# An attention and MLP kernel on one core: planner thresholds set for each half group of score blocks, and a new order of instructions

## The chip, the core and the metric

The kernel runs on one core of one Trainium2 chip. Its engines work side by side, each on its own list of instructions: TensorE (PE in the profile; its weight loads are PEld), VectorE (DVE), ScalarE (ACT), GpSimd (POOL) and SyncE (SP), which starts transfers. The metric is the time in device microseconds of one launch; 746.28 us is the median of three runs before the change.

## What is computed

The reference mixes an attention block A and an MLP block B of the same input `x` (1 x 2048 x 640, bf16) by a gate:

```python
def _A_ref(x, wqkv, wo):
    B, S, D = x.shape
    H = 32; Dh = D // H
    qkv = (lambda x, *d: x.transpose(*d))((x @ wqkv).reshape(B, S, 3, H, Dh), 2, 0, 3, 1, 4)
    q, k, v = qkv[0], qkv[1], qkv[2]
    scale = Dh ** -0.5
    scores = jnp.einsum("bhqd,bhkd->bhqk", q, k) * scale
    p = _softmax(scores, axis=-1)
    o = jnp.einsum("bhqk,bhkd->bhqd", p, v)
    return (lambda x, *d: x.transpose(*d))(o, 0, 2, 1, 3).reshape(B, S, D) @ wo

def _B_ref(x, w1, b1, w2):
    h = jnp.einsum("bsd,df->bsf", x, w1) + b1
    sp = jnp.log1p(jnp.exp(-jnp.abs(h))) + jnp.where(h > 0, h, jnp.zeros_like(h))
    act = h * jnp.tanh(sp)
    return jnp.einsum("bsf,fd->bsd", act, w2)

x = A_x
g = _sigmoid((x * gate_w).sum(-1, keepdims=True))
return g * _A_ref(x, A_wqkv, A_wo) + (1 - g) * _B_ref(x, B_w1, B_b1, B_w2)
```

The 32 heads have 20 dimensions each; the MLP is 640 to 1536 to 640 with the Mish function.

## The kernel before

**Tiles.** Four heads form a quad, and 512 queries a column block. A group (`GROUPS`, L52) is one quad with one column block: 8 x 4 = 32 groups, the first 24 quad by quad, the last 8 (quads 6 and 7) column block by column block. A group has 64 score blocks: 16 stretches of 128 keys for each of four heads, each block 128 keys by 512 queries, so 2,048 blocks in all. A half group is 32 blocks.

**One block.** TensorE computes its scores with one matmul on 32 of the array's rows (a head's 20 dimensions, padded), into one of seven PSUM banks (`emit_score`, through `mm`, L506, whose call stands at L507 in the profile). One to four blocks, one for each row tile, go out side by side as a score group. The exponential is then taken in one of two ways:

- ScalarE takes one, two or three neighbouring banks in one instruction and writes bf16 into one, two or three of the 34 slots of `E` (L1312).
- VectorE takes one bank and writes, as 16-bit integers, a straight line that reads as a power of two in bf16 (`psum_chord`, L1345). Two more terms with other offsets are then derived from it (`line`, L1363), two blocks at a time: by GpSimd (`poll_gp`, L1512), or by VectorE where GpSimd has much to do (`run_x`, L1367). The sum of the three terms stands for the exponential. Such a block therefore occupies three slots of `E`, and its product with V takes three matmuls in place of one.

PV matmuls use 32 of the array's columns, one column tile for each of the quad's four heads, and add up in the eighth bank (`emit_pv`, L1000). Up to four go out side by side as a PV group. V has columns of ones, so the same sum gives the softmax denominator. When a group is complete, VectorE copies the bank out (L1406); its denominators go through DRAM and back, and GpSimd multiplies (L1620).

**Other work.** The transposes of `x`, the projections, the MLP and the output projection are cut into pieces (`Misc`) with due times in units of half groups. They run in TensorE's column shape in between, use the same seven banks, and are mostly evacuated by VectorE.

**What sets the order.** `make_plan` (L422) plays the kernel through with a clock of assumed costs. Whenever an engine is free, its poll function chooses what it does next: `poll_pe` (L1156) tries scores, then PV when few slots of `E` are free, then pieces that are due soon, then PV, then other pieces, and in the end `fill` (L1184), four matmuls with zero weights into the bank of sums. `poll_act` (L1225) chooses the banks for ScalarE, `poll_dve` (L1382) the block for VectorE. The choices depend on thresholds in `PAR`: how many blocks a score group must have (`vk`, `idlek`), when it may be smaller (`thr`, `lead`, `hold`), how much GpSimd may have queued when VectorE begins a new pair (`gpmax`), when a derived term goes to VectorE (`xmin`, `xwait`, `xb`), when ScalarE takes three banks (`a3gp`), how long a PV is held after its exponential (`slack`, in `late`, L1200), how many banks pieces may hold (`mb`), and others.

`late_par` (L877) gives a threshold its value: one before block 591 (`ph`), another (`thr_2` and so on) from there on. `elow`, `urgent` and `swait` have one value throughout.

The plan yields 5,440 steps. `ORDER` (L124) is a fixed text, three hexadecimal digits for each step, that says in which order these steps are written out; `unpack` (L262) reads it and the loop at L1773 emits them. Nothing else orders the engines: each runs its own list, and semaphores between them follow from what the steps read and write.

Of the kernel before, what the change touches and what calls it, by code (L numbers as in the profile page):

```python
# [52 lines left out]
for _c in range(NQC):  # L53
    GROUPS += [(6, _c), (7, _c)]
NG = len(GROUPS)
NU = NG * 64
# [39 lines left out]
    "wo": 23.808422394577885,  # L96
    "thr_2": 337.7597040015291,
# [19 lines left out]
for _k in ("thr", "lead", "gpmax", "xmin", "xwait", "vk", "a3gp", "dahead", "age", "ahd", "hold", "idlek", "mb", "dvw", "slack", "mgb", "xb"):  # L117
# [7 lines left out]
    "007000000000000000000000000000000000000000005000000000000000000000000000000000000000000000000000000000000000000000000000001000"  # L125
    "000000000000000000000000000001000000002001000000000000000000000000001000000000000000000000001000000000000001000000000000001000"
# [4 lines left out]
    "00900800a00000000a00b00000000000000000100300000000d00000400100200300500600700800a00e009000002000002001000001000000003004006002"  # L131
    "00500700800000900b00a00c00d00e00800f01001301401601501201701901801101b01c01e01d01f00000600800700900a00b00c00d00e00f010016014013"
    "01201501a00000800a00000500000a00000200000200000000d000001003002000002001000000003001000004003000006001000006002003005007001000"
    "00500000200500b00000200000200400000600500700200900a00800d00c00b01000e01301101601201501701800f01901b01a01d01c01e01f020021023024"
    "02202502702802a02902c02f02e02b03003703503403303103a03603803903b02d03c03d04003f041042032044053000033032031000022023025027024029"
    "02802a02b02c02e02f03003103203303403803700002101d02302202402502602702802d02a03003102c00002402d02a03002e029031026039033032034035"
    "03600002e02f03403503203703603803903300002a02d02c03002e02f02103303103503a03403203c00002002102200000e01001400000100600500800400b"
    "00700c00300e00a00901001200d00f01501101300000300400500600800700900b00a00c00d00e01201001100001401101201301501901601b00000a01200b"
    "01301100f00000700800000600800900b00a00700d00c00e01001100f01201500000300400000500000400500900e00301000000500600800000000200000c"
    "00300600500b00e00a00900800700f01c01101001201301401601701501901801b01d01f01a01e00001401301a01901801501b016017000000000000000000"  # L140
    "00000100300700500800000a00c00800900b00400000d00b00c00f00500000400800000300000400300e00800900600a00700b01600d01000f011000000001"
    "00000000300200700600900000800900000a00500300600000700000300600100a00200800400f000005002007009000008000000000000001000000000000"
    "00500200000000100000100200000000100000200100000000100000100000100000100000000600100800400000900100a00500800c00300701001300b000"
    "00100000000000000200300900600a00b00c00d00e00101001101301401500000301300101501601b01701400e00401801901a01201c000012013000000001"
    "00300600800000c00800500200a00b00701001100d00e01401500f01301601701801a01201c01d01902702001b02202402301f02502802601e02a02102c02d"
    "02e03002f03202903403503703303803603a03b03c03102b03e03f03904104004404604504704804a04c04e04204d03d04f04905105204b043054053057056"
    "05005905505800005905805a05c05705d06305f06005b06205e06506106406706806a06606906d06c06f06e07007207107507707607307807d07a07c07f079"
    "08208106b08008408508308708807b08a08908b08608e09008d09209409308c08f07409609500009609109409209307809509c09809909a09d0970a309b000"
    "01701300000600500c00000f00700900a00601100801600d01201300c01701801000101f01501b01a01401c02401e02000001400000800a00c00d00e00f000"
    "00c000000000000000001008000000000005003002001006000003002006001004000003004000000000000000000000001000006009001005008002004007"  # L150
    "00d00c00b00e01100a01201301401900f00001300000700800000600700500800900b00a00d00e00c000001000002000003002004006009005019007000002"
    "00400600500300800900700d00a00e00f01401200000100800a00b00c00f00501000e00d00000300800200100500700600d00900f00a01000c00000700e00a"
    "00d01000f012011013000003000000000002001000000001000000000001000000000000000000001000000000000000000000000000000000000000002001"
    "00000100000000000100300400600000300600000000100400200300000000300100200400600a00800c00900500b00d00000b00700800d00a000003005007"
    "006000000002001000000000000000000000001002005003004000001000001000002001003000004000005002004006007000007000002001000000001000"
    "00000000000100200300500400a00900800700d00c00e00600f01101201001601401501701801a01e01b01301c01d02002301f02201902100001901c01a01e"
    "01d02001f02300000600701400900a00c00d00f00e01000b01600000200800100400000400300500100600900700a008000000002006003001005007008009"
    "00a00e00b00c00d01000f01101701201301601901801a01b00001b01a00000800900c00f01100e00d010000012011015016014013017018000000000000000"
    "00100200500400300600700d00c00b01100e00801000f01201301401601501b01702001a01801c01f01d01e02101902302400902502202602802702902c02b"
    "02d02e03002f03103302a00002a02b02e02d03003203303102c00000c00e00f00d01101001301400000e01301100000700b00c00a00501000400d000000001"  # L160
    "00000000000100300500000200600800700500900b00a00c00e00f01000d01201101501401601800001501601700000900000800700a00900600c00b00d010"
    "00f00e01100000000200000000200100300000100000200b00000200300500400700600800e00d00b00c00f00901101201501301401601701901801b01a01d"
    "01c02102001e01f02302502202602400001801701901c01b01e01d02200000500600700902c00a00d00c01400000400600500300800700a00b00c01300e00d"
    "01001401201101500000700000000000100000100300200f00500700001d00500600701000900002300602500002200d00400500e01002d00000100000601b"
    "00200901c00b00100001200700a00001e00700900601602d00b02302401801701902601b02502803402902a02b00c00a01d02c03a01203002e01f02f03c022"
    "02000002900702b01f00000001b00001701501801d01601c01a01e01f02102302202002402602802502700001801902001a01c01d01e01f021022023025024"
    "00000f00c00d00e01001101601201301401501701b01c01901a01802501d01f02302002202602401e02802102702902a02f02b03402e03102c02d030032036"
    "03803503304003c03a03904403b03d03e00003403b03703803a03c04103d02c04204000000e00800d01201301101601700901501400f010000000005001004"
    "00200300800600000300000200300000200100600000200500600000000400900000200000000c00001201400600000701400800000000d001009000014000"
    "00800400600b00700d00f01401501001701600000100a00000d00000300100000100200300000000800f001002011000001014003000003005016004006000"  # L170
    "00600000200000000500c00700d00300100600001701901800000200500100000000200400500100300700600800d00c000005000009000001009000004002"
    "00000600000000700a00000f000001000000000013004005003001006007000003004002000001000007000000000000000000005002003000000000001002"
    "000002000006007000001000010001000001000000000004002001003000000001000003001000000000001002000000000000000001000000002000000000"
    "00000000000100000000500000100200300000000000000200500100300700400000000000000000000000000000300100900c00e005006010008002015019"
    "00b00d00700f00000600d00e00000100800300a00400f00000200400c00600700b00d01100e00000700800b00a00c00f00e00d011013010015012000013017"
    "01501601e01802201901b01c01a00000200300a00400700c01000d00b00f01100600e01701200801301401601801c01901a00001401201601701801d01901a"
    "02101c00001200f01401801601701e01a01301f01901d01b000013017000000000001002000000001000000000001002005004003006000000000000002001"
    "00000000000000000000000000100000200100000400100200300500000000100200000200100000100800300600400900700500b00e00f00d00c010011012"
# [243 lines left out]
def make_plan(K, par):  # L422

    pl = Clock()
# [375 lines left out]
    for c in range(NQC):  # L800
        for f in range(FT):
            k = c * FT + f
# [74 lines left out]
    def late_par(k):  # L877
        return par[k + "_2"] if nxt[0] >= par["ph"] else par[k]
# [277 lines left out]
    def poll_pe():  # L1156
# [649 lines left out]
```

## Time and profile before

| | |
|---|---|
| median of three runs | 746.28 us (745.99 to 746.67) |
| the profiled execution | 747.05 us |
| its span, first to last instruction | 745.1 us |
| score blocks whose exponential ScalarE takes | 1,464 |
| score blocks on VectorE | 584 |
| derived terms (two blocks each) on GpSimd, on VectorE | 431, 153 |
| PV matmuls | 3,216 |

How to read the rows that follow in the prediction. A row of a group names its line, engine, operation, the tiles written and read, their shapes and the count; after the bar stands the time in which at least one of them ran and the mean of one in ns; after the second bar the idle time of the engine just before them, and what ended it. Matmuls that run side by side on different row or column tiles overlap, so a mean of 383 ns is the length of one and not the distance to the next. That distance is read from the rows in order of time, whose first two columns are the start and the length in us; neighbouring matmuls of one form are merged in one row with their count. `E,VA` are PV matmuls, `qT,kT` scores, `xT,zero` fill. A row by stretches gives, after the stretch and its length, the busy us and number of instructions of each engine.

### The profile page before, as it was taken

The page shows a single profiled execution, that of the slowest core. Times are in us where ns is not written, and L with a number is a line of the kernel's source. Part 1 is how long each engine was busy: PE and PEld are TensorE (multiplying, and loading weights), DVE is VectorE, ACT ScalarE, POOL GpSimd, SP SyncE. Part 2 cuts the span into 40 slices and gives each one's busy share as a digit, 9 for nine tenths or more (in the row PEclk, how much of TensorE's full clock was granted, in tenths as well). Part 3 has the DMA queues.
Part 4 walks back from the last instruction along what each step waited for, and adds up shares of the span by engine and source line. Part 5 has one row for each costly group of instructions (what it writes and reads, how often), then busy time and mean ns, then how long its engine had stood idle before and what let it go on. Part 6 is the DMA issues. An engine that isn't in the chain of part 4 may idle for free.

```text
span 745.1 us, 24873 instructions
## 1 busy us (share of the span) xinstructions
PE 729.6 (98%) x10332; PEld 255.2 (34%) x10332; DVE 607.1 (81%) x1047; ACT 713.2 (96%) x750; POOL 521.9 (70%) x501
## 2 busy tenths in 40 slices
PE   8999999999999999999999999999999999999997
PEld 4433343333235333333332222223433333333333
DVE  4688888888979797988788878887878788797876
ACT  6899989999999999999999999999999999999995
POOL 9466735565578557667676587687986788797884
PEclk9999999999999999999999999999999999999999
DMA  9611120011011000112102211130111111211202
GB/s 284 199 48 54 50 82 17 20 52 39 17 29 60 16 29 26 50 44 74 39 28 59 54 43 50 39 101 21 43 52 39 39 38 39 71 60 60 72 21 86
DMA packets 45720, 41.82 MB, mean 56 GB/s; under 512 B 20120, under 2 KB 39240, under 8 KB 45608
## 3 DMA queue, kind: packets, MB, share of 16 engines
q1 hardware_dynamic: 42984, 39.94, 17.8%
q8 instruction: 80, 1.31, 0.7%
q10 hardware_dynamic: 2624, 0.31, 0.3%
q14 instruction: 32, 0.26, 0.1%
HBM read 27.59 MB, written 12.38 MB: 54 GB/s over the span
## 4 chain that ended last, share of the span: by engine, by line
PE 80%; ACT 10%; DVE 7%; issue 2%; POOL 0%; DVEq 0%; ACTq 0%; POOLq 0%
PE ps L507 80%; ACT E L1312 9%; DVE E L1347 4%; DVE E L1365 2%; DVE accs L1406 0%; POOL E L1365 0%; ACT act L1236 0%; PE ps L1753 0%; PE ps L520 0%; ACT xT L528 0%; ACT L1236 0%; DVE bst L656 0%; DVEq L1801 0%; DVE qT L544 0%; DVE ost L689 0%
## 5 line engine op out<-in xcount | busy, mean ns | idle before, releaser
L1312 ACT ACTIVATE E<-ps 128x1024 bf16<-128x1024 f32 (+2 forms) x723 | 680.0, 1070 | 19.3 <-PE ps L507 16.4
L1365 POOL TENSOR_SCALAR E<-E 128x1024 uint16<-128x1024 uint16 x431 | 457.8, 1063 | 209.7 <-DVE E L1347 155.0
L1347 DVE TENSOR_SCALAR E<-ps 128x512 uint16<-128x512 f32 x584 | 388.8, 684 | 94.1 <-PE ps L507 85.6
L507 PE MATMUL ps<-E,VA 128*32 128x512 bf16 x3216 | 299.4, 383 | 1.7 <-DVE E L1347 0.6
L507 PE MATMUL ps<-qT,kT 32*128 32x512 bf16 x2048 | 284.0, 384 | 5.3 <-ACT E L1312 2.6
L507 PEld LDWEIGHTS <-kT 32*128 32x128 bf16 x2048 | 75.3, 91 | 261.3 <-issue 257.2
L507 PEld LDWEIGHTS <-VA 128*32 128x32 bf16 x3216 | 78.9, 95 | 97.5 <-issue 78.2
L1365 DVE TENSOR_SCALAR E<-E 128x1024 uint16<-128x1024 uint16 x153 | 97.9, 643 | 2.0
L507 PE MATMUL ps<-R,act 128*32 128x320 bf16 x1536 | 87.1, 302 | 0.4 <-ACT act L1236 0.4
L507 PE MATMUL ps<-xT,R 128*32 128x512 bf16 x960 | 82.4, 383 | 0.0
L507 PEld LDWEIGHTS <-R 128*32 128x32 bf16 (+1 forms) x1728 | 40.8, 95 | 44.7 <-issue 34.0
L507 PEld LDWEIGHTS <-act 128*32 128x32 bf16 x1536 | 36.4, 95 | 32.1 <-issue 22.2
L637 DVE TENSOR_SCALAR act<-ps,b1f 128x512 bf16<-128x512 f32 x48 | 35.7, 744 | 7.4 <-PE ps L507 6.6
L507 PE MATMUL ps<-wv,xT 128*32 128x241 bf16 (+2 forms) x720 | 37.6, 276 | 0.5 <-DVE E L1347 0.3
L507 PE MATMUL ps<-wk,R 128*32 128x320 bf16 (+1 forms) x640 | 37.5, 303 | 0.2
L507 PE MATMUL ps<-xT,wq 128*32 128x512 bf16 x400 | 34.8, 383 | 0.1
L507 PE MATMUL ps<-xT,wk 128*32 128x512 bf16 (+1 forms) x360 | 34.7, 384 | 0.0
L1620 POOL TENSOR_TENSOR ons<-accs,rb 128x512 bf16<-128x512 f32 x24 | 31.5, 1310 | 1.8 <-DVE E L1347 0.7
L567 DVE CAST stg<-ps 128x512 bf16<-128x512 f32 (+1 forms) x40 | 27.3, 683 | 5.1 <-PE ps L507 4.9
L507 PEld LDWEIGHTS <-xT 128*32 128x32 bf16 (+1 forms) x720 | 19.6, 96 | 13.0 <-issue 9.4
L1406 DVE COPY accs<-ps 128x512 f32<-128x512 f32 x31 | 21.2, 684 | 1.3 <-PE ps L507 1.0
L1236 ACT ACTIVATE act<-act 128x3072 bf16<-128x3072 bf16 x8 | 21.5, 2752 | 0.0
(72 smaller groups left out, 190.3 us busy)
## 6 DMA issues: line engine op xcount, KB each, us to landing
rb<-rd_d SPq DMA_DIRECT2D x124, 64.0 KB
qd<-stg SPq DMA_DIRECT2D x20, 128.0 KB
b_d<-bst SPq DMA_DIRECT2D x16, 160.0 KB
out_dram<-ost SPq DMA_DIRECT2D x16, 160.0 KB
kT<-kd SPq DMA_DIRECT2D x28, 80.0 KB
qT<-qd SPq DMA_DIRECT2D x28, 80.0 KB
stg<-b_d SPq DMA_DIRECT2D x13, 160.0 KB
kd<-stg SPq DMA_DIRECT2D x16, 128.0 KB
```

The costliest lines, as they stand in the source:

```text
L507: K.nc.tensor.matmul(o, lhsT=l, rhs=r, start=first, stop=last, tile_position=pos, skip_group_check=True)
L567: K.nc.vector.tensor_copy(out=K.stg[0:w, s, :], in_=bank(b)[0:w, :])
L637: K.nc.vector.tensor_scalar(out=K.act[:, f, (c % 2) * QC : (c % 2 + 1) * QC], in0=bank(b), scalar1=K.b1f[:, f : f + 1], scalar2=None, op0= ...
L1236: K.nc.scalar.activation(a, a, ACT.Mish)
L1312: lambda: K.nc.scalar.activation(K.E[:, e : e + w, :], K.ps[:, b0 : b0 + w, :], ACT.Exp, scale=SCALE)
L1347: lambda: K.nc.vector.tensor_scalar(out=K.E[:, e + h, :].bitcast(U16), in0=K.ps[:, b, :], scalar1=CH_MUL, scalar2=CH_OFF + CH_ADD[0], op0= ...
L1365: eng.tensor_scalar(out=o, in0=i, scalar1=float(CH_ADD[k]), scalar2=1.0, op0=ALU.add, op1=ALU.mult)
L1406: emit(lambda: K.nc.vector.tensor_copy(out=K.accs[:, g % 2, :], in_=K.ps[:, ACCB, :]))
L1620: gp_q.append((1350.0, lambda: K.nc.gpsimd.tensor_tensor(out=dst(), in0=K.accs[:, b, :], in1=K.rb[:, b, :], op=ALU.mult), lambda: pl.give( ...
```

## The change

`PAR` gets a table `win` with one entry for each half group from 0 to 62, each with 19 thresholds. `late_par` looks up the half group that the next score block belongs to (`nxt[0] // 32`), goes back to an earlier one if there is none, and uses the values of before only where the table has none (`mgb` alone). `elow`, `urgent` and `swait` are now read through `late_par` too. `ORDER` is replaced; the plan has 5,519 steps. All functions that write instructions are as they were.

```diff
@@ PAR @@
+    "win": {
+        0: {"thr": 311.433, "lead": 183.566, "gpmax": 3438.02, "xmin": 2062.55, "xwait": 144.133, "vk": 3, "a3gp": 1688.88, "dahead": 387.745, "age": 6.22086, "ahd": 8.57763, "hold": 5, "idlek": 7, "mb": 9, "dvw": 69.8524, "slack": 141.973, "xb": 3, "elow": 20.6823, "urgent": 22.6857, "swait": 211.87},
...
+        30: {"thr": 125.838, "lead": 56.4012, "gpmax": 6719.54, "xmin": 2767.26, "xwait": 124.546, "vk": 3, "a3gp": 5844.89, "dahead": 236.954, "age": 7.03157, "ahd": 3.79319, "hold": 0, "idlek": 5, "mb": 7, "dvw": 158.838, "slack": 44.9159, "xb": 0, "elow": 48.3964, "urgent": 12.8156, "swait": 91.9349},
...
+        62: {"thr": 103.466, "lead": 46.6119, "gpmax": 6719.54, "xmin": 2590.39, "xwait": 132.388, "vk": 3, "a3gp": 10617.2, "dahead": 223.929, "age": 9.63641, "ahd": 4.29725, "hold": 3, "idlek": 4, "mb": 9, "dvw": 283.517, "slack": 73.7542, "xb": 0, "elow": 60.7258, "urgent": 27.9078, "swait": 75.8091},
+    },
@@ late_par @@
-        return par[k + "_2"] if nxt[0] >= par["ph"] else par[k]
+        w = nxt[0] // 32
+        while w >= 0:
+            if k in par["win"].get(w, ()):
+                return par["win"][w][k]
+            w -= 1
+        return par[k + "_2"] if k + "_2" in par and nxt[0] >= par["ph"] else par[k]
@@ poll_pe @@
-        if len(efree) <= par["elow"] and try_pv():
+        if len(efree) <= late_par("elow") and try_pv():
...
-        if try_misc(par["urgent"]):
+        if try_misc(late_par("urgent")):
@@ poll_act @@
-                if len(at) + len(fl) > 1 and nxt[0] < NU and pl.t < idle_since[0] + par["swait"]:
+                if len(at) + len(fl) > 1 and nxt[0] < NU and pl.t < idle_since[0] + late_par("swait"):
@@ ORDER @@
...
```

More of the change, by code (lines that the diff above doesn't have):

```diff
@@ L124 @@
 ORDER = (
[L125 to L126 removed]
+    "007000000000000000000000000000000000000000000004000000000000000000000000000000000000000000000000000000000000000000000000001000"
+    "000000000000000000000000000001000000002001000000000000000000000002000000000000000000000000001000000000000001000000000000001000"
     "000000000000000000000000000000000001000000000000000000000000000001000000000000000000000000000000000000000000000000000000000000"
@@ L134 @@
[L134 to L137, printed above, removed]
@@ new lines @@
+    "00300600500000500300400700800900600a00d000001004006005007000005000003005004000000000003006000001004000003000001002005004007006"
+    "00000500600800700c00000400000000000000100000100000300500000700000200400700500c00a00f00000300600d00000d00000400500600700300a011"
+    "000000000000005001002000002003000006001000001000001000000002001000000001000000000000000002003000000000000000001009002000009007"
+    "00000300000000200500000000000000200000400200300600c00000000000100200000000100000000000000a002000002003004006007005000000000001"
@@ new lines @@
+    "00200300000000000000400200600300b00c00500800700900a00d00e00101101000f01a01300000200500600400300700900a00b00c00d01000e00f011012"
+    "01300000100200400500000000000000000400000100400601400200000000200000000000100200000100000600000200600900400700800b00a00c00f000"
+    "00f00c00d01001101201301401501601701901c01a01b000008005006007000000002001005004008000003004000001003002004005000002001004003005"
+    "000000000000000000001002000000001000000000000001003000004002000000000000001002003004000007001003005000008006004000005008000002"
@@ new lines @@
+    "006004005000000000000001000000001002000000002003000003000001003002000000000001000000005001002003006000000003000007000000000000"
+    "00100400000500700400f00800900a00b01300c01400e01000000f01400001501601201700000c01501901101601700701801a01c01b01d01e01f020022023"
+    "02502602700000800900a00000900800a00000700900a00800c00b00d00f00e010011013012015016014017018000001002000001003000002003004005000"
+    "00100200300400000200100400500300600700900a00800b00c01100e00000200500300700800900a00000000200500000300200600700a00900b00500f008"
@@ new lines @@
+    "01000d01201501101801601301900000b01000801201400e01100f01301701602201a01901c01d01801e01b02002102402301f02602900002302a025028000"
+    "01601301801e01901f01c01b01d01a02002202302802600000800b00300900a01000c00e00d00f01101300001001101d012014000011015014013017018020"
+    "01601e01c01901d01a01f02102202402600001701b01c01d01e01f021020022019023000001000001003002006005004007008009000002001013003004000"
+    "00201100100400c00000000300200500100000400b00600700000700c00a00800d00e00000a00500600800900701900b00e01200000c00b000001000000000"
@@ new lines @@
+    "00100000100200900500600b00800400700a00d00c00000100200900000300100200000000000000400300200100000200100000c000000001004003005006"
+    "002000000000000000002001003006005007009000004006009008000003007005006008000000000000003000000002000000002000003002004000000001"
+    "000002000000000000000000000000000000001000001000003001006002004005000000000000000000000001000001000001000004001003000005003004"
+    "00600800700900a00b00c00d00f00e000000001005004002003006007000000002000000001000006000001000000000000001000000001002000000000000"
@@ new lines @@
+    "000001002000000000000000000000000000000000000000000000000000000000000000001002000003001002000000000000002001000000000000000000"
+    "00000000000000000100000000500100000100200600400500800700a00900b00c00e00000200000000100000100900200500400600700a00800c00000800a"
+    "00c00000000000000200000500200300400000200300b00100400000500000300100200600000000100300000000000100400500300600900800700a000009"
+    "000002001000000000001004002000002005004006003007008009000001002004000000000000002003005004000005000002003006001004000002003004"
@@ L255 @@
+    "00000000000300200400600501900801a00700900a00d00c00b00f00e00001501101600f01b01a00000700000c00000100000500900800a00d00100e00f011"
+    "00601300000400000e00000500a000000002003000000000000"
 )
```

280 lines of the change are left out of this document (160 added, 120 removed).

## The prediction

> **What bounds the kernel now.** I read the page first (busy shares, slices, chain), then the busy time by stretches, the matmul order in time, the waits, and the groups of instructions. The page:
>
> ```profile
> span 745.1 us, 24873 instructions
> PE 729.6 (98%) x10332; PEld 255.2 (34%) x10332; DVE 607.1 (81%) x1047; ACT 713.2 (96%) x750; POOL 521.9 (70%) x501
> PEclk9999999999999999999999999999999999999999
> PE 80%; ACT 10%; DVE 7%; issue 2%; POOL 0%; DVEq 0%; ACTq 0%; POOLq 0%
> ```
>
> TensorE is busy for 98% of the span and carries 80% of the chain that ended last; ScalarE is close behind. The stretches, cut where the 1st, 129th, 1,665th and last of the 2,048 score blocks start (columns: length, then busy us of each engine with its instruction count, granted clock, DMA share, GB/s):
>
> ```profile
> 0.00:10.40 10.40, 7.83 (x94) 4.36 (x95) 3.10 (x9) 3.86 (x6) 9.73 (x22) 1.00 0.87 284
> 10.40:60.10 49.70, 48.91 (x666) 20.11 (x665) 35.66 (x77) 46.54 (x51) 30.78 (x32) 1.00 0.46 142
> 60.10:606.50 546.40, 542.80 (x7674) 182.79 (x7670) 455.63 (x769) 534.69 (x559) 373.33 (x347) 1.00 0.15 44
> 606.50:731.70 125.20, 121.68 (x1742) 42.77 (x1739) 104.94 (x178) 123.85 (x130) 103.42 (x98) 1.00 0.18 55
> 731.70:745.10 13.40, 8.38 (x168) 5.17 (x164) 7.78 (x17) 4.29 (x7) 4.64 (x5) 1.00 0.21 75
> ```
>
> From 60.1 to 606.5 us TensorE is idle for 3.6 us of 546.4: there it is the bound, and ScalarE has 11.7 us to spare. From 606.5 us on ScalarE is the busiest (123.85 of 125.2). So what counts is how long TensorE's list of work takes, and the trace shows what one piece of it costs:
>
> ```profile
> 399.72 0.62 PE L507 MATMUL ps<-xT,wk 128*32 128x512 bf16 x8
> 400.16 0.39 PE L507 MATMUL ps<-E,VA 128*32 128x512 bf16 x4
> 400.48 0.39 PE L507 MATMUL ps<-qT,kT 32*128 32x512 bf16 x3
> 400.81 0.61 PE L507 MATMUL ps<-xT,wk 128*32 128x512 bf16 x8
> 401.35 0.39 PE L507 MATMUL ps<-qT,kT 32*128 32x512 bf16 x2
> 401.67 0.61 PE L507 MATMUL ps<-xT,wk 128*32 128x512 bf16 x8
> 402.22 0.40 PE L507 MATMUL ps<-qT,kT 32*128 32x512 bf16 x4
> 402.54 0.40 PE L507 MATMUL ps<-xT,wk 128*32 128x512 bf16 x4
> 402.77 0.39 PE L507 MATMUL ps<-E,VA 128*32 128x512 bf16 x4
> 403.09 0.39 PE L507 MATMUL ps<-qT,kT 32*128 32x512 bf16 x2
> ```
>
> Take differences of starts. Eight column matmuls (two sets of four side by side) to the next set: 400.16 - 399.72 = 0.44, so 0.22 us a set. A score group (row tiles, `qT,kT`) to what follows: 0.33, 0.32, 0.32 us for three, two and four matmuls: it costs the same however many of its four row tiles are filled. From a set of PV (`E,VA`) to scores also 0.32. So every group of 512 columns costs 0.22 us, and every change between the score shape and the column shape 0.10 us more. Nothing else waits in these 4 us.
>
> **The change part by part.** The engines' programs differ in order and in counts, not in the forms of their instructions. The counts below come from the two programs' own order; the prices from these groups of the trace (columns: line, engine, operation, shapes, count, busy us, mean ns, idle before):
>
> ```profile
> L1312 ACT ACTIVATE E<-ps 128x1024 bf16<-128x1024 f32 x675 | 632.1, 1060 | 16.1 <-PE ps L507 13.4 <-POOL E L1365 0.5 <-ACT E L1312 0.3
> L1365 POOL TENSOR_SCALAR E<-E 128x1024 uint16<-128x1024 uint16 x431 | 457.8, 1063 | 209.7 <-DVE E L1347 155.0 <-PE ps L507 19.3 <-ACT E L1312 6.6
> L1347 DVE TENSOR_SCALAR E<-ps 128x512 uint16<-128x512 f32 x584 | 388.8, 684 | 94.1 <-PE ps L507 85.6 <-ACT E L1312 2.3 <-issue 0.6
> L507 PE MATMUL ps<-E,VA 128*32 128x512 bf16 x3216 | 299.4, 383 | 1.7 <-DVE E L1347 0.6 <-DVE E L1365 0.4 <-DVE accs L1406 0.4
> L1365 DVE TENSOR_SCALAR E<-E 128x1024 uint16<-128x1024 uint16 x153 | 97.9, 643 | 2.0
> L1312 ACT ACTIVATE E<-ps 128x1536 bf16<-128x1536 f32 x33 | 48.8, 1478 | 0.8 <-PE ps L507 0.6
> L507 PE MATMUL ps<-xT,zero 128*32 128x512 bf16 x112 | 9.9, 382 | 0.0
> L1312 ACT ACTIVATE E<-ps 128x512 bf16<-128x512 f32 x15 | 9.4, 628 | 2.5 <-PE ps L507 2.4
> ```
>
> *Blocks moved to VectorE.* 584 become 636. ScalarE's instructions over two, three and one blocks go from 675, 33 and 15 to 687, 4 and 26. By busy time over count (0.936, 1.479, 0.627 us): +11.2 - 42.9 + 6.9 = -24.8 us of ScalarE. VectorE gets 52 x 0.666 = 34.6 us and three more derived terms at 0.640, +1.9: 607.1 becomes about 643.6. GpSimd's derived terms go from 431 to 480: 49 x 1.062 = +52.0, 521.9 to about 574. A block on VectorE needs three PV matmuls instead of one, so these rise by 104, 3,216 to 3,320. That is the change's cost on the bounding engine: 26 full sets, 5.7 us at 0.22, if all were full.
>
> *They are not full sets only.* PV groups before: 869, of which 735 have all four column tiles; after: 878, of which 770 do. A partial group costs the same 0.22, so 104 more matmuls cost 9 groups, +2.0 us.
>
> *Score groups.* With one to four blocks: 19, 169, 457, 80 before, 15, 122, 515, 61 after: 725 become 713, -12 x 0.22 = -2.6 us.
>
> *Fill groups* (zero weights, L1184's `fill`): 28 become 12, -16 x 0.22 = -3.5 us. They stand where the planner saw TensorE with nothing to do, so this is a gain only if real work stands there now.
>
> *Changes of shape* between scores and columns: 1,356 become 1,318, -38 x 0.10 = -3.8 us.
>
> *All other matmuls* (projections, MLP, output) and all of SP's DMAs are the same in number; only their place moves. The sum on TensorE: 2.0 - 2.6 - 3.5 - 3.8 = -7.9 us.
>
> *Where it falls.* The last 384 blocks have 1 score group and 7 PV groups more, 12 fills fewer, as many changes of shape, and 17 more pieces of output projection. Such a piece has 320 columns:
>
> ```profile
> 610.54 0.72 PE L507 MATMUL ps<-R,act 128*32 128x320 bf16 x16
> 611.20 0.39 PE L507 MATMUL ps<-qT,kT 32*128 32x512 bf16 x3
> ```
>
> Four of them and a change take 0.66, so one takes 0.14. The stage gets -4 x 0.22 + 17 x 0.14 = +1.5 us, the part behind the last score +0.5 (7 pieces more, a group and two changes fewer), and the first 1,664 blocks the rest, -9.9. In the last stage ScalarE was the bound; it goes from 117 pairs and 11 triples to 127 pairs and none, with 3 more singles: 10 x 0.936 - 11 x 1.479 + 3 x 0.627 = -5.0, 123.85 to about 118.9, while TensorE goes to 121.68 + 1.5 = 123.2 and VectorE (+10 blocks, +12 derived terms) to 104.94 + 6.7 + 7.7 = 119.3. Three engines then stand within 5 us of each other, so I give that stage nothing.
>
> *Waits.* What TensorE and its neighbours wait for now (total us, times, longest us):
>
> ```profile
> DVE E L1347 <- PE ps L507: 85.6, 179, 2.6
> ACT E L1312 <- PE ps L507: 16.4, 27, 3.7
> PE ps L507 <- ACT E L1312: 2.8, 9, 0.6
> PE ps L507 <- DVE E L1347: 2.1, 6, 0.6
> ```
>
> TensorE's named waits on the exponentials are 4.9 us in all; VectorE waits for TensorE, not the other way. A ScalarE with 24.8 us less to do frees banks earlier, so part of these 4.9 us can go; the added VectorE work and new thresholds that let PV follow its exponential more closely (the planner's `slack` falls from 121 ns to between 42 and 85 in all but three half groups) can add some. Bounds: all of TensorE's 7.1 us of idle between 60.1 and 731.7 goes (-7), or the 3.5 us of the removed fills come back as idle (+3.5). I take -1, nearer to the named waits than to either end. Span: 745.1 - 7.9 - 1 = 736.2 us. The profiled execution took 747.05, 1.95 above its span, and the median of the runs is 746.28, 0.77 below that: 736.2 + 1.95 - 0.77 = 737.4 us.
>
> *GpSimd and VectorE together.* One row speaks against moving more there:
>
> ```profile
> L1365 DVE TENSOR_SCALAR E<-E x153: 408/461/1479, 24.4 to 731.5; 128x1024 uint16<-128x1024 uint16 x153
> ```
>
> Minimum, median, maximum ns: the same VectorE operation takes 408 or up to 1,479, mean 643 by its group, so 235 ns of it on average are waiting inside the instruction. With GpSimd's busy share going from 70% to 574/736 = 78%, I scale: 235 x 78/70 = 262, +27 ns x 156 = +4.2 us of VectorE, not on the bounding engine. The Trainium skill ("SBUF — State Buffer", Who interferes with whom) says that GpSimd and a VectorE instruction in a 2-port mode share one port pair under an exclusive lock, so that the second blocks until the first is done. The spread of the row agrees; by that rule an operation that meets a GpSimd one at random waits half of its 1.06 us, an estimate of 0.53 x 0.78 = 0.41 us, which would be 0.15 more than the scaled row and 23 us more VectorE time over 156 of them; the median of 461 says that most of them meet none.
>
> **The rivals.** *The fills come back as idle* (0.16): the 16 removed groups stood in real waits and the waits stay. For it: ScalarE was the bound where they stood. Against it: 17 real pieces of work now stand in the last stage. Gain 7.9 - 3.5 = 4.4 without the -1: 741.9 us.
>
> *Both bounds give way* (0.12): ScalarE's 24.8 us also take the idle of TensorE away, -7.9 - 5 = -12.9: 733.4 us. For it: from 606.5 us on the chain runs through ScalarE. Against it: VectorE at 119.3 us there.
>
> *VectorE becomes the bound in the last 384 blocks* (0.11), the case on the other side. Now it is idle there for 125.2 - 104.94 = 20.3 us. If this idle is inherent (a block cannot start before its scores land, and nothing is queued to fill in), the stage takes 119.3 + 20.3 = 139.6, +14.4 us; with -9.9 and +0.5 that is +5.0: 751.3 us. It decides from the point where more than 15.3 of the 20.3 us remain. For it: 179 waits of VectorE on scores. Against it: these are waits of an engine with time to spare; evacuations and derived terms can move into them.
>
> *The clock falls without the fills* (0.02). The clock row shows 9 in all slices with 28 fills. The only slow matmuls are the first ones:
>
> ```profile
> L1753 PE MATMUL ps<-wkp,zero 128*32 128x512 bf16 x24 | 2.8, 627 | 1.3 <-DVE wkp L1736 1.3
> ```
>
> 627 ns each instead of 383. If each of the 16 removed groups cost one stretch like this one, 2.8 us of work that would take 1.3, it would be +24 us: 746.28 + 24 - 4.4 = 766 us. Against it: no wait of TensorE above is longer than 0.6 us. The Trainium skill ("TensorE: Matmul & The Clock Gate", What's actually happening) gives about 3.4 us without work as what halves the clock; no row here has such a gap after the start.
>
> **How the numbers follow.** The forecast has 0.59 and its own range is 734 to 740. The range reaches below to 7.9 + 7 us of gain (731.4) and above past the returned fills (741.9) to 744.5, which leaves room for 2.5 us of new waits, half of today's 4.9; the VectorE case lies mostly outside. A measurement of this kernel tells 0.2%, 1.5 us, from no change. Faster: 0.59 + 0.16 + 0.12 = 0.87, of which 0.01 may shrink to nothing. The VectorE case ends within 0.2% in 0.02 of its 0.11, so same has 0.03, and slower 0.09 + 0.02 = 0.11.
>
> **What would show it.** Right: TensorE busy falls by about 7 us to 722 to 724 and stays above 98% of a shorter span; ScalarE's busy time falls to about 690; VectorE's rises to 640 to 650 without naming itself in TensorE's waits; the stretch between blocks 129 and 1,664 shortens by 8 to 11 us and the last 384 blocks by no more than 3. Wrong: TensorE's idle time grows past 25 us, with `PE ps <- DVE E` or `<- ACT E` at more than 10 us; or the last stage grows past 130 us with VectorE above 95% in it. The price of 0.10 for a change of shape is wrong if TensorE's busy time doesn't fall though the counts do.

## The result, and the profile after

The changed kernel takes 736.75 us (median of four runs, 734.53 to 739.12) against 746.47 for the kernel before beside it: ratio 0.9869, 95% interval 0.9835 to 0.9902, a gain of 9.7 us with bounds of 7.3 and 12.3. The prediction was 737.4. The profiled execution is the fastest of the four, 734.53 us.

The page after, busy time and share of each engine, and the shares of the chain that ended last:

```profile
span 732.7 us, 25066 instructions
PE 718.0 (98%) x10372; PEld 255.8 (35%) x10372; DVE 633.2 (86%) x1102; ACT 694.4 (95%) x744; POOL 572.3 (78%) x550
PE 83%; ACT 7%; DVE 7%; issue 2%; DMA 1%; POOL 0%; SPq 0%; DVEq 0%; ACTq 0%; POOLq 0%
```

TensorE and ScalarE lost 11.6 and 18.8 us of busy time, VectorE and GpSimd gained 26.1 and 50.4. TensorE's idle time, span less busy, is 14.7 us after 15.5. The stretches, cut at the same score blocks as before (1st, 129th, 1,665th, last):

```profile
0.00:10.20 10.20, 7.58 (x94) 4.23 (x95) 3.12 (x9) 3.93 (x6) 9.53 (x22) 1.00 0.85 282
10.20:59.20 49.00, 47.96 (x625) 19.44 (x624) 35.92 (x78) 45.80 (x50) 32.20 (x33) 1.00 0.49 152
59.20:593.80 534.60, 530.56 (x7674) 181.94 (x7670) 470.52 (x798) 518.15 (x551) 423.62 (x398) 1.00 0.16 43
593.80:719.20 125.40, 122.70 (x1805) 44.18 (x1801) 116.38 (x202) 122.13 (x133) 101.56 (x95) 1.00 0.20 58
719.20:732.70 13.50, 9.18 (x190) 6.00 (x187) 7.29 (x17) 4.36 (x7) 5.44 (x6) 0.96 0.28 93
```

Of the 12.4 us of span, 11.8 come from blocks 129 to 1,664 (546.4 to 534.6); the last 384 blocks take 125.4 instead of 125.2, the part behind the last score 0.1 more. The waits after (total us, times, longest), and the derived terms and blocks on VectorE and GpSimd:

```profile
DVE E L1419 <- PE ps L574: 55.7, 137, 1.2
ACT E L1384 <- PE ps L574: 18.9, 41, 3.7
PE ps L574 <- DVE E L1419: 2.4, 5, 1.0
PE ps L574 <- ACT E L1384: 1.9, 6, 0.5
```

```profile
L1437 POOL TENSOR_SCALAR E<-E 128x1024 uint16<-128x1024 uint16 x480 | 508.2, 1060 | 148.4 <-DVE E L1419 101.8 <-PE ps L574 14.8 <-ACT E L1384 4.7
L1419 DVE TENSOR_SCALAR E<-ps 128x512 uint16<-128x512 f32 x636 | 421.3, 683 | 63.4 <-PE ps L574 55.7 <-ACT E L1384 0.7 <-issue 0.6
L574 PE MATMUL ps<-E,VA 128*32 128x512 bf16 x3320 | 301.8, 383 | 1.6 <-DVE E L1437 0.9 <-DVE accs L1478 0.7
L1437 DVE TENSOR_SCALAR E<-E 128x1024 uint16<-128x1024 uint16 x156 | 97.3, 624 | 1.5
```

The 52 more blocks went into VectorE's idle time: its idle before blocks fell from 94.1 to 63.4 us, and its wait for scores from 85.6 to 55.7. TensorE's waits for VectorE and ScalarE did not grow (4.9 to 4.3).

### The profile page after: what moved, and what is told of

The parts are those of the page before. It is cut to its first block, busy times and chain, and to the rows that moved or that the text cites. A ratio compares the mean times of both kernels' runs of the same rounds, so it can differ in the third digit from the quotient of the medians.

```text
span 732.7 us, 25066 instructions
## 1 busy us (share of the span) xinstructions
PE 718.0 (98%) x10372; PEld 255.8 (35%) x10372; DVE 633.2 (86%) x1102; ACT 694.4 (95%) x744; POOL 572.3 (78%) x550
## 4 chain that ended last, share of the span: by engine, by line
PE 83%; ACT 7%; DVE 7%; issue 2%; DMA 1%; POOL 0%; SPq 0%; DVEq 0%; ACTq 0%; POOLq 0%
PE ps L574 83%; ACT E L1384 7%; DVE E L1419 3%; DVE E L1437 2%; DMA act<-in_A_x_dram 1%; DVE act L704 0%; DVE ost L818 0%; DVE bst L723 0%; POOL E L1437 0%; PE ps L587 0%; ACT xT L595 0%; DVE qT L611 0%; PE ps L1620 0%; DVE accs L1478 0%; DVE og L1341 0%
## 5 line engine op out<-in xcount | busy, mean ns | idle before, releaser
L1384 ACT ACTIVATE E<-ps 128x1024 bf16<-128x1024 f32 (+1 forms) x717 | 660.9, 1035 | 22.5 <-PE ps L574 18.9
L1437 POOL TENSOR_SCALAR E<-E 128x1024 uint16<-128x1024 uint16 x480 | 508.2, 1060 | 148.4 <-DVE E L1419 101.8
L1419 DVE TENSOR_SCALAR E<-ps 128x512 uint16<-128x512 f32 x636 | 421.3, 683 | 63.4 <-PE ps L574 55.7
L574 PE MATMUL ps<-qT,kT 32*128 32x512 bf16 x2048 | 278.9, 384 | 5.8 <-DVE E L1419 2.2
L574 PEld LDWEIGHTS <-kT 32*128 32x128 bf16 x2048 | 73.3, 90 | 252.8 <-issue 248.7
L574 PEld LDWEIGHTS <-VA 128*32 128x32 bf16 x3320 | 82.4, 95 | 99.4 <-issue 79.3
L574 PEld LDWEIGHTS <-R 128*32 128x32 bf16 (+1 forms) x1728 | 42.7, 95 | 43.9 <-issue 33.6
L574 PEld LDWEIGHTS <-xT 128*32 128x32 bf16 (+1 forms) x720 | 18.9, 96 | 12.9 <-issue 9.8
```

Source lines behind the costliest of these rows:

```text
L574: K.nc.tensor.matmul(o, lhsT=l, rhs=r, start=first, stop=last, tile_position=pos, skip_group_check=True)
L1384: lambda: K.nc.scalar.activation(K.E[:, e : e + w, :], K.ps[:, b0 : b0 + w, :], ACT.Exp, scale=SCALE)
L1419: lambda: K.nc.vector.tensor_scalar(out=K.E[:, e + h, :].bitcast(U16), in0=K.ps[:, b, :], scalar1=CH_MUL, scalar2=CH_OFF + CH_ADD[0], op0= ...
L1437: eng.tensor_scalar(out=o, in0=i, scalar1=float(CH_ADD[k]), scalar2=1.0, op0=ALU.add, op1=ALU.mult)
```

## The experiments

The profiled executions of these 14 programs start their first score 10.2 to 17.2 us after the first instruction (told of below). So beside the median and the ratio to the kernel before, this table has the profiled execution's time from the first score to the end, and its difference to the kernel it was made from. That time is one execution each, and it has chance in it too: between the start of the 137th and the 141st score the kernel before loses 0.5 us to each of before_no_fill, before_pe_less and before_act_less, and the first two have left out nothing by then. So a difference of half a microsecond says nothing, and these three differences are 0.5 us too favourable. The medians were taken in four sittings, each with its own runs of the kernel before, so they are compared by their ratios.

| run | median us | ratio to before | 95% | first score at | from there to the end | difference |
|---|---|---|---|---|---|---|
| before | 746.47 | 1 | | 10.4 | 734.7 | |
| changed | 736.75 | 0.9869 | 0.9835 to 0.9902 | 10.2 | 722.5 | -12.2 |
| plan_order_before | 752.19 | 1.0078 | 1.0049 to 1.0107 | 10.4 | 739.5 | +4.8 to before |
| plan_order_after | 739.97 | 0.9902 | 0.9870 to 0.9935 | 11.5 | 726.6 | +4.1 to changed |
| win_first_52 | 741.71 | 0.9915 | 0.9885 to 0.9945 | 13.4 | 727.3 | +0.7 to plan_order_after |
| pe_more_columns | 743.65 | 0.9961 | 0.9932 to 0.9989 | 10.3 | 730.5 | +8.0 to changed |
| pe_more_rows | 749.51 | 1.0033 | 1.0012 to 1.0055 | 14.9 | 735.2 | +12.7 to changed |
| act_more | 744.30 | 0.9958 | 0.9944 to 0.9972 | 12.3 | 731.9 | +9.4 to changed |
| dve_more | 756.98 | 1.0118 | 1.0094 to 1.0143 | 10.4 | 743.1 | +20.6 to changed |
| dve_more_small | 738.49 | 0.9888 | 0.9861 to 0.9915 | 11.0 | 725.4 | +2.9 to changed |
| before_no_fill | 748.75 | 1.0012 | 0.9993 to 1.0030 | 15.4 | 733.2 | -1.5 to before |
| after_no_fill | 734.86 | 0.9822 | 0.9795 to 0.9850 | 12.1 | 721.8 | -0.7 to changed |
| before_act_less | 742.69 | 0.9941 | 0.9915 to 0.9967 | 17.2 | 728.7 | -6.0 to before |
| before_pe_less | 747.54 | 0.9995 | 0.9978 to 1.0012 | 10.4 | 734.4 | -0.3 to before |

The theory at the start: TensorE's list of work is the bound, and the gain is its 7.9 us. The rival: ScalarE's relief of 24.8 us is the gain. A third question is which half of the change, thresholds or order, carries it.

### Thresholds or order

```diff
-    for i in unpack(ORDER):
+    for i in range(len(plan["pl"].fns)):
```

Both kernels, steps written out as the planner made them.

> The changed kernel's plan, with its steps written out in the planner's own order instead of ORDER. Counts of instructions and shape changes of the plan are nearly the same, the searched order is gone. If the gain comes from the new plan (my theory: 7.9 us less work on TensorE), it stands close to the changed kernel, 737 to 742 us, and clearly below the kernel before in its own planner order. If the gain comes from the order search, it falls back to 745 us or more.

> The kernel before, its steps in the planner's own order. Together with the run beside it this splits the change: the difference of these two is what the thresholds are worth, the rest is the order. Plan theory: 8 to 11 us above the changed plan in planner order. Order theory: the two are within 3 us of each other.

In planner order the two are 12.9 us apart (739.5 and 726.6; by the ratios 1.0078 - 0.9902 = 1.76%, 13.1 us). The searched order is worth 4.8 us in the kernel before and 4.1 in the changed one. So the thresholds carry the whole gain, a little more than I expected, and the new search brings no more than the old one did.

### Which half groups

```diff
+for _w in range(52, 63):
+    PAR["win"].pop(_w)
+PAR["win"][52] = {_k: PAR[_k + "_2"] for _k in _keys}
+PAR["win"][52].update({_k: PAR[_k] for _k in ("elow", "urgent", "swait")})
```

The last 384 blocks get the thresholds of before (`_keys` are the 16 names with a second value), steps in planner order.

> The changed kernel's table for half groups 0 to 51 only; the last 384 blocks planned with the thresholds of before, all in planner order. Its TensorE list costs 494.1 us by 0.22 a group and 0.10 a change (scores, PV and fills), against 493.8 for the whole table and 502.3 for none. By that it stands within 1 us of the changed plan in planner order (739 to 742 us). If the thresholds of the last stage carry the gain, above 745 us.

0.7 us above the whole table in planner order, as expected by the price of its list. The last 11 half groups' thresholds are worth next to nothing: the stage that gained nothing in the trace is also the one that can do without its new values.

### More work for TensorE, in both shapes

```diff
+    pvn = {}
+
+    def zeros():
+        for r in range(4):
+            mm(K.ps[32 * r : 32 * r + 32, ACCB, :], K.zero, K.xT[:, 0, 0:QC], False, False, (0, 32 * r))
...
         emit(fn)
+        pvn[g] = pvn.get(g, 0) + 1
+        if 2 <= g < 26 and pvn[g] in (12, 16):
+            emit(zeros)
```

and in the other run, on zero weights of 32 rows by 128 columns:

```diff
+    def zeros():
+        mm(K.ps[:, ACCB, :], K.zrow[0:32, :], K.xT[0:32, 0, 0:QC], False, False, (0, 0))
...
```

> The changed kernel with 48 more groups of zero-weight matmuls in the column shape, two in each of groups 2 to 25, each right behind a PV group, so no change of shape is added. They leave the result as it is. 48 x 0.22 = 10.6 us of TensorE work. If TensorE is the bound there, +7 to +10.6 us (its 4 us of idle in that stretch can take some): 744 to 747 us. If ScalarE is the bound and TensorE has time to spare, 0 to +3 us.

> The same 48 places with one zero-weight matmul in the score shape instead of four in the column shape. 24 of the places stand ahead of a column matmul, so they add two changes of shape each; 24 stand ahead of scores and add none. 48 x 0.22 + 24 x 2 x 0.10 = 15.4 us: 4.8 us above the column version, 748 to 752 us. If a change of shape cost nothing of its own, or a group cost by its number of matmuls (one for four), it would be equal to the column version or below it.

The column version costs 8.0 us of its 10.6 (6.9 by the ratios, just under the expected range), the row version 12.7. Their difference is 4.7 us where 24 x 2 x 0.10 = 4.8 was expected. TensorE's order in time in the row version shows one of the added matmuls:

```profile
76.83 0.40 PE L574 MATMUL ps<-E,VA 128*32 128x512 bf16 x4
77.16 0.39 PE L574 MATMUL ps<-xT,zrow 32*128 32x512 bf16 x1
77.47 0.40 PE L574 MATMUL ps<-E,VA 128*32 128x512 bf16 x4
77.80 0.39 PE L574 MATMUL ps<-qT,kT 32*128 32x512 bf16 x3
```

One matmul in the score shape takes 0.31 us to the next start, as three do behind it in the prediction's rows (0.32). The price of a change of shape holds, and of added TensorE work three quarters show in the time, so an added group costs 0.17 of its 0.22 us. That is the theory's side of the matter. It says what added work costs, not what removed work gains.

### More work for ScalarE

```diff
+            if sum(stat["act%d" % q] for q in (1, 2, 3)) % 3 == 0:
+                emit(lambda: K.nc.scalar.activation(K.dmy, K.dmy, ACT.Copy))
```

> The changed kernel with a tiny ScalarE instruction (copy of one column onto itself) behind every third exponential: 239 of them at about 0.11 us each, some 26 us, which gives back the 24.8 us that the change took off ScalarE. If TensorE's work was the gain, ScalarE's spare time takes part of it and the kernel stays below the one before: 737 to 743 us. If ScalarE's relief was the gain, all of it is lost: 745 to 750 us.

744.3 us lies between the two expectations: +6.6 by the ratios, +9.4 from the first score. How much was added is read from the rows in order of time, here one copy and the exponentials behind it:

```profile
304.76 0.23 ACT L1389 ACTIVATE dmy<-dmy 128x1 f32<-128x1 f32 x1
304.85 2.88 ACT L1384 ACTIVATE E<-ps 128x1024 bf16<-128x1024 f32 x3
```

From its start to the next exponential a copy takes 0.09 us here (0.10 behind others), so 239 of them are 22 to 24 us and not quite the 26 of the expectation; ScalarE's busy time from the first score on rose by 15.2 us only (690.4 to 705.6), since its neighbouring instructions overlap. Neither theory alone; ScalarE has time to spare, but not 22 us of it. This shook the first theory, and the next two runs take each relief by itself in the kernel before.

### Each relief alone

Less ScalarE:

```diff
+            n = QC - 21 if full_once.issuperset(range(e, e + w)) else QC
+            full_once.update(range(e, e + w))
             emit(
                 lambda: K.nc.scalar.activation(
-                    K.E[:, e : e + w, :], K.ps[:, b0 : b0 + w, :], ACT.Exp, scale=SCALE
+                    K.E[:, e : e + w, 0:n], K.ps[:, b0 : b0 + w, 0:n], ACT.Exp, scale=SCALE
...
+    full_once = set()
```

> The kernel before, with every exponential instruction of ScalarE (but the first into each slot of E) over 491 instead of 512 columns of each bank; the last 21 columns of these blocks are left as they were. About 4% of 690 us, some 26 us less of ScalarE, and TensorE's list untouched: the change's relief of ScalarE alone. If ScalarE's relief was the gain, 735 to 739 us. If TensorE's list was, only the last 384 blocks (where ScalarE was busiest) and small waits gain: 742 to 746 us.

Less TensorE:

```diff
+    left_out = []
...
+        skip = len(items) == 1 and not todo[0][4] and not todo[0][5] and g >= 2 and len(left_out) < 36
+        if skip:
+            left_out.append(g)
+
         def fn():
+            if skip:
+                return
```

> The kernel before without 33 of its PV groups that fill one column tile only; 33 blocks' terms are left out of the sums. 33 x 0.22 + 8 changes of shape x 0.10 = 8.1 us less of TensorE, the three other engines untouched: the change's relief of TensorE alone. If TensorE's list was the gain, 738 to 741 us. If TensorE only waits for ScalarE in the end, 744 us or more.

The relief of ScalarE alone gives 4.4 us by its ratio and 6.0 from the first score (5.5 without the half microsecond of chance): more than the small waits, less than the whole. How large the relief was is known only roughly, from the group of shortened pairs:

```profile
L1314 ACT ACTIVATE E<-ps 128x982 bf16<-128x982 f32 x658 | 604.8, 995 | 17.8 <-PE ps L507 11.7 <-ACT E L1314 0.7 <-issue 0.6
```

The mean of one fell from 1,060 to 995 ns (43 us over 658), the busy time over count only from 936 to 919 (11 us). The shortest distance from the start of one pair to the start of the next fell from 903 to 869 ns in the trace, 22 us over 658, and this is the fairest of the three; the 26 us of the expectation lie near it. The relief of TensorE alone gives next to nothing (0.9995; 0.3 us from the first score), against the theory. This run's stretch from the first score to the end, and TensorE's waits in it:

```profile
10.40:744.80 734.40, 717.23 (x10205) 250.20 (x10204) 601.86 (x1039) 708.96 (x744) 513.92 (x480) 1.00 0.18 53
```

```profile
PE ps L507 <- ACT E L1320: 5.3, 15, 0.6
PE ps L507 <- DVE E L1355: 3.1, 9, 0.8
```

From the first score on TensorE is busy for 717.2 us, 4.6 less than before (721.8, the sum of the prediction's last four stretches), and idle for 17.2 instead of 12.9. Its named waits on the exponentials rise from 4.9 to 8.4 us. Most of the removed work has turned into waiting.

The 0.3 us hide two things, which show when the starts of the scores are compared one by one with the kernel before. By the 1,941st score the run is 1.8 us ahead, 1.3 without the half microsecond of chance. By the 1,973rd it has lost 1.5 of it, because the granted clock fell to half for 3.4 us (shown in the last section). So the 33 groups are worth 1.3 us of the expected 8.1, 0.04 each, and the price of the fallen clock comes on top.

Where these groups stand is told by the planner's code. In the kernel before all 46 groups of one column tile go out by the ordinary `try_pv`, the same that sends full ones; it lets a PV group be smaller when the other heads of the quad have no block left in this column block. So they are the last blocks of a quad's column block, and not work that is only sent when all else has failed. The next quad or column block can't use the bank of sums before this one is complete, so TensorE has no other PV in stock there. That this is why it waits for the exponentials there is argued from the code and not shown.

### The fills

```diff
-        emit(fn)
+        emit(lambda: None)
         stat["fill"] += 1
```

> The kernel before without its 28 fill groups; nothing else is moved. I counted 0.22 us for each removed fill. If they cost real time, 28 x 0.22 = 6.2 us less: 740 us. If they stand in waits that stay, no change, within 1 us of 746.5. If the clock needs them, a granted clock below 1.0 after 520 us and some us more.

> The changed kernel without its 12 fill groups. If fills cost real time, -2.6 us: 734 us. If they stand in waits, no change, 736 to 738 us. If the clock needs them, the clock of its runs falls below the 0.997 to 0.999 of the changed kernel and its times spread more.

Without its 28 fills the kernel before gains 1.5 us from the first score on. The half microsecond of chance is in it and stands long before the first fill (at 527 us), so 1.0 us is left, 0.04 each and not 0.22; its median doesn't tell from no change. TensorE is busy 4.9 us less there and idle 3.4 more:

```profile
15.40:748.60 733.20, 716.89 (x10127) 248.95 (x10126) 601.24 (x1039) 708.79 (x744) 507.74 (x474) 1.00 0.18 51
```

The clock in this row is 1.00 without a single fill, so in this execution fills are not what holds it. Only one execution is traced. Over all ten the mean granted clock is 0.992 to 1.0, beside 0.996 to 1.0 for the kernel before, and where the others lost it is not known. The changed kernel without its 12 fills is the fastest of all (734.86 us, and 721.8 from the first score), but its interval overlaps that of the changed kernel, and from the first score on it gains 0.7 us: at most a small gain.

### More work for VectorE

```diff
+        if stat["dve"] % 4 == 0:
+            emit(lambda: K.nc.vector.tensor_copy(out=K.dmv[:, 0:64], in_=K.dmv[:, 64:128]))
...
```

and in the other run

```diff
+        if stat["dve"] % 4 == 0:
+            emit(lambda: K.nc.vector.reciprocal(out=K.dmv, in_=K.dmv))
...
```

> The changed kernel with a small VectorE copy (64 fp32 columns) behind every fourth block that VectorE takes: 159 of them at 0.1 to 0.15 us, 16 to 24 us. If VectorE has time to spare (my theory), +0 to +4 us. If VectorE at 86% of the span is already the next bound, its added time shows in full in the last 384 blocks (31 of them, 3 to 5 us) and in part before: +8 us or more.

> The same 159 places as in the run with small VectorE copies (which cost 20 us), now with a reciprocal of 16 columns, about 0.16 us each, 25 us, with no wait on GpSimd expected inside it. If the loss came from the copies and GpSimd's operations holding each other up, it shrinks to 8 us or less: below 745 us. If VectorE's time itself stands on the path, 15 to 25 us: 752 to 761 us.

The copies cost 20.6 us, the reciprocals in the same places 2.9. The added operations by their tile (minimum, median, maximum ns) and as a group (busy us, mean ns), first the copies, then the reciprocals:

```profile
L1540 DVE COPY dmv<-dmv x159: 172/203/1067, 27.4 to 739.0; 128x64 f32<-128x64 f32 x159
```

```profile
L1540 DVE COPY dmv<-dmv 128x64 f32<-128x64 f32 x159 | 61.4, 386 | 0.0
```

```profile
L1540 DVE RECIPROCAL dmv<-dmv x159: 230/242/246, 28.0 to 722.0; 128x16 f32<-128x16 f32 x159
```

```profile
L1540 DVE RECIPROCAL dmv<-dmv 128x16 f32<-128x16 f32 x159 | 38.3, 241 | 0.0
```

The copy is the shorter operation (172 ns at best) but takes up to 1,067; the reciprocal always takes about 242. The copies' busy time is 23.1 us above the reciprocals' and the run's time 17.7. The Trainium skill ("SBUF — State Buffer", Who interferes with whom) says that a VectorE copy can enter a 2-port mode in which it and GpSimd block each other for a whole instruction; the spread of the copies agrees with that, and this kernel's GpSimd is busy for 76% to 78% of the time with instructions of 1.06 us in the mean. That the lock is the whole cause isn't shown; no run took GpSimd's work away. VectorE at 86% had room for the 159 reciprocals at 2.9 us of run time. Its whole busy time rose by only 12.6 us with them (633.2 to 645.8), since they overlap their neighbours, and by 36.5 with the copies (to 669.7).

## Why the prediction was right, and where its reasons were not

**The time.** 8.9 us of gain were forecast and 9.7 measured. The place was right too: 8 to 11 us were forecast between blocks 129 and 1,664 and 11.8 came in the profiled execution, nothing in the last 384 (+0.2). That the sum came so near is in part luck, since terms that were too large and one that was too small made up for each other, as told below.

**The prices.** Added work confirmed 0.10 us for a change of shape (4.7 us against 4.8 for 48 changes) and 0.17 of the 0.22 for a group. What removed changes of shape and score groups are worth was not tried. TensorE's busy time fell by 11.6 us, more than the 7 foreseen, to 718.0 and not to 722 to 724.

**What failed: that TensorE's list is the bound, so that each group taken off it is worth its price.** The terms mis-sized by that are the fills (-3.5 us for 16; by the kernel before without fills 28 are worth 1.0, so 16 some 0.6) and the PV groups that are not full: 33 of them left out gave 1.3 us of the expected 8.1. The prediction's +2.0 for PV is 35 full groups more (+7.7) and 26 smaller ones fewer (-5.7); at 0.04 us each the smaller ones give back only 1.0, and the term becomes +6.7. Most of the time of such groups comes back as waiting when they are left out. The profile's 98% contains them.

**What was undersized: ScalarE's relief,** to which I gave 1 us. Shorter exponentials, some 26 us by the expectation, gave 5.5 us alone, and some 26 us more by the same counting cost the changed kernel 9.4. The change takes 24.8 us off: 24.8/26 of these two are 5.2 and 9.0 us. With that, the shape changes (-3.8), score groups (-2.6), PV groups (+6.7) and fills (-0.6) add up to between -5.5 and -9.3, beside the -12.2 from the first score to the end. So the sum doesn't close, and how the gain divides between the two engines stays open. What is shown is that the thresholds carry it, that less ScalarE work alone gains, and that the TensorE groups that were left out gain little. Both reliefs together in the kernel before, the run that would show whether they are worth more than their sum, were not tried.

**The rivals.** Returned fills: the price of the fills did fall away, but other terms made up for it, so the time did not go to 741.9. Both bounds giving way (733.4 forecast): in its mechanism the nearest to what the runs show, though the median ended nearer to the forecast. VectorE as the bound in the last 384 blocks: its idle time there fell from 20.3 to 125.4 - 116.38 = 9.0 us, well below the 15.3 at which it would have decided; wrong. The clock without fills: it held at 1.00 in the traced execution without any. But the reason given against this rival, that no wait of TensorE is longer than 0.6 us, isn't enough: in before_pe_less, with all fills, the clock fell behind waits of at most 0.52 us.

**GpSimd and VectorE.** I scaled the wait inside VectorE's derived terms from 235 to 262 ns; the mean is 624 with a minimum of 408, so 216. By the mean the new thresholds place them no worse although GpSimd is busier; the median rose from 461 to 508. What such waits can cost was seen only when copies were added that the plan didn't know of.

**VectorE's busy time** came to 633.2, not 643.6, and ScalarE's fell by 18.8, not 24.8: sums over groups count time twice where neighbouring instructions of different groups overlap. The groups' means held (683 ns a block, 0.937 us a pair).

## What to carry to other kernels

An engine at 98% isn't shown to be the bound: test with less work as well as with more, since 10.6 us more TensorE work cost 8.0 us and 8.1 us less gained 1.3. Look for work that stands where the engine would wait anyway (fills, the last PV of a quad's column block). Where two engines are both above 95%, ask what less work for each is worth by itself before the gain is put down to one. The cost of the third engine that takes the work is read from its idle time and from whether its operations lengthen beside another engine's, not from its busy share. Where runs differ by some us, compare from the first instruction of the steady part, and block by block: here this found half a microsecond of chance and a fall of the clock that a sum over the whole run hid.

## What the runs showed of the hardware that was not expected

The profiled executions differ by up to 7.0 us in when the first score starts. In the kernel before without fills the first score came at 15.4 us instead of 10.4; its start by stretches, then its waits there:

```profile
5.00:10.00 5.00, 0.97 (x17) 0.71 (x14) 0.90 (x2) 2.06 (x4) 5.00 (x8) 0.82 1.05 381
10.00:15.40 5.40, 5.40 (x54) 2.52 (x53) 1.52 (x3) 0.00 (x0) 5.40 (x8) 0.53 1.08 325
```

```profile
PE ps L507 <- ACT xT L528: 3.6, 1, 3.6
ACT wqp L477 <- DMA wq<-in_A_wqkv_dram: 2.9, 1, 2.9
```

A load of weights that landed late held ScalarE for 2.9 us and through it TensorE for 3.6; the granted clock then fell to 0.82 and 0.53 of full speed in the two stretches, and the first projections ran at that. Such a start costs 5 us though the load itself was less than 3 late, and it comes in kernels with and without fills (first score at 17.2 us in before_act_less, 14.9 in pe_more_rows, which has all of its fills and 48 groups more). The Trainium skill ("TensorE: Matmul & The Clock Gate", What's actually happening) gives about 3.4 us without work as what halves the clock; the 3.6 us wait agrees, but shorter waits were followed by a fall too. In act_more no wait of TensorE in the start is longer than 1.3 us, and the clock was 0.73 between 5 and 10 us.

In before_pe_less the clock fell in the middle of the kernel, with all fills in place. TensorE's rows in order of time, then the two stretches around the fall:

```profile
690.33 0.44 PE L507 MATMUL ps<-qT,kT 32*128 32x512 bf16 x4
691.30 0.65 PE L507 MATMUL ps<-qT,kT 32*128 32x512 bf16 x4 [0.52 <-ACT E L1320]
692.21 0.39 PE L507 MATMUL ps<-qT,kT 32*128 32x512 bf16 x3 [0.27 <-ACT E L1320]
693.13 0.40 PE L507 MATMUL ps<-qT,kT 32*128 32x512 bf16 x3 [0.52 <-ACT E L1320]
693.45 0.83 PE L507 MATMUL ps<-E,VA 128*32 128x512 bf16 x12
694.22 0.87 PE L507 MATMUL ps<-qT,kT 32*128 32x512 bf16 x4
```

```profile
691.00:694.40 3.40, 2.31 (x23) 0.70 (x23) 3.40 (x7) 3.40 (x5) 3.32 (x4) 1.00 0.75 237
694.40:697.90 3.50, 3.50 (x31) 0.81 (x29) 1.90 (x4) 2.70 (x4) 2.90 (x3) 0.51 0.03 4
```

Three waits for ScalarE of 0.27 to 0.52 us came close together, so TensorE was busy for 2.31 of 3.40 us; then the clock was at 0.51 for 3.5 us, and the run lost 1.5 us against the kernel before. Here no gap came near 3.4 us. Where the page and this trace differ, the trace counts: several short waits in a row can be followed by a fall of the clock. Which share of waiting it takes isn't shown.
